# An attention kernel's item loads, with each row of 6144 or 4672 bytes cut into two rows of 3072 or 2368

## The chip, the core and the metric

The program runs on one core of one Trainium2 chip. A core has a matrix engine (PE, with its weight loads shown apart as PEld), a vector engine (DVE), a scalar engine (ACT), a general engine (POOL) and a sequencer that mostly issues transfers (SP). Sixteen DMA engines carry all transfers between the device memory and the on-chip buffers. The metric is the device time of one execution in microseconds (us), taken as the median of the runs.

## The reference

Two blocks follow each other. The first is a linear attention with a decaying state, over 4 batches, 8 heads, 768 tokens and 48 values per head:

```
for t in range(S):
    kt, vt, rt = k[:, :, t], v[:, :, t], r[:, :, t]
    cur = einsum('bhd,bhe->bhde', u * kt, vt)
    y[:, :, t] = einsum('bhd,bhde->bhe', rt, state + cur)
    state = w * state + einsum('bhd,bhe->bhde', kt, vt)
```

The second takes y as x (4 x 768 tokens of 384 values), chooses one of 8 experts for each token by a gate (a token may keep the expert of the token before it), and returns p[e] * (relu(x @ w1[e]) @ w2[e]), where w1 is 384 x 1024 and w2 is 1024 x 384. All is float32.

## The kernel before

The attention takes 16 items, one for each batch and pair of heads (4 x 4). The two heads of an item lie on partitions 0 to 47 and 64 to 111. An item's 768 tokens are six chunks of 128. What an item needs from device memory comes in three loads, which `load(n)` issues on SP's queue:

- `rk`: r and k with the head's values on the partitions and the tokens along them, 128 partitions x 2 x 768 values;
- `kv`: k and v with the tokens on the partitions, 128 partitions x 576 values each and 16 values of padding;
- `vT`: v in a third layout, 128 x 768 values.

Four buffers hold rk and vT, five hold kv. `load(n + 3)` is written ahead of the work of item n, so three items are loaded or under way while one is computed. The loads of items 0, 1 and 2 stand at the very start, those of item 3 follow once the loop begins. Item 0's rk comes in two loads of half the chunks each (L202), every other rk in one (L199); kv is L203, vT is L204. Eight completion counters are used in turn for SP's loads, so an issue also waits until the load eight places before it has landed.

The order of the work on each engine is written by hand in `run`. The steps of an item n, with the lines by which the profile names them:

- POOL, in `scale(n)`: `ke` (L217, k of kv times a table of decays), `rw` (L234, r of rk times decays) and `pd` (L221, r times k), each in two halves. For items 0 to 2 the order is pd, ke and DVE makes rw; from item 3 it is ke, rw, pd. `scale(n + 1)` is issued during item n.
- DVE: `kw` (L241, k of rk times inverse decays), the multiplication of a score by a mask into `am` (L290), the scan over chunk states `S` (L259), the product with vT in `own` (L273), and for the first items two steps L157 and L158 that prepare the inverse decays.
- PE: `added` (L253, ke against v into the bank `mp`), `inside` (L297, am against v), `before` (L310, rw against S), `scores` (L288, rw against kw), `own` (L269, pd summed), `turn` (L323, transposes of the finished item).
- ACT copies results out of the banks (L314, L325) and stores four batches of x to device memory (L328).

After the last load SP fetches the first expert's weights (L1024, L1026). Then ten blocks of tokens run through the experts; PE is busy almost without a break there. Their loads (1536 KB each, rows of 12288 bytes) and the gathers and scatters of tokens on POOL do not touch the tensors of the change.

Of the kernel before, what the change touches and what calls it, by code (L numbers as in the profile page):

```python
# [50 lines left out]
C2 = NCH // 2  # L51
AHEAD = 4
VB = NCH * 2 * DH


def spread(ap, axis, n):
# [5 lines left out]
class Attention:  # L62
# [13 lines left out]
    def __init__(self, tc, st, rk_d, kv_d, vT_d, x_d, w_t, wp_d, kept, ident, lt, mp):  # L76
        self.tc, self.nc = tc, tc.nc
        nc = tc.nc
        self.rk_d, self.kv_d, self.vT_d, self.x_d = rk_d, kv_d, vT_d, x_d
        self.w_t, self.kept, self.ident, self.lt = w_t, kept, ident, lt  # L80

        self.late = st.enter_context(tc.tile_pool(name="late", bufs=1))
        self.wp = self.late.tile([P, H, 32], F32, name="wp")
        self.sel = self.late.tile([P, 2 * (E + 1)], F32, name="sel")
        self.inner = ExitStack()

        def pool(name, bufs, **kw):
            return self.inner.enter_context(tc.tile_pool(name=name, bufs=bufs, **kw))

        once = pool("once", 1)  # L90
        self.two = pool("two", 2)
        self.three = pool("three", 3)
        ps = pool("ps", 1, space=PSUM)

        self.pairs = [ps.tile([P, 2, 512], F32, name=f"pair{i}") for i in range(2)]
        self.py = pool("py", 1, space=PSUM)

        self.T = mp[:, 2 * P + 2:2 * P + 2 + (NCH - 1) * DH].rearrange("p (e c) -> p e c", c=NCH - 1)

        self.inv = pool("pinv", 1, space=PSUM).tile([P, HP, P], F32, name="inv")  # L100


        n = B * HP - 1
        self.rks, self.vTs = [None] * AHEAD, [None] * AHEAD
        for i in range(1, AHEAD + 1):
            self.rks[(n + i) % AHEAD] = once.tile([P, 2, NCH, P], F32, name=f"rk{i}")
        for i in range(1, AHEAD + 1):
            self.vTs[(n + i) % AHEAD] = once.tile([P, 2, C2, P], F32, name=f"vT{i}")
        self.kvs = [once.tile([P, 2 * VB + DP - DH], F32, name=f"kv{i}") for i in range(AHEAD + 1)]
        self.items = [dict() for _ in range(B * HP)]  # L110
        self.xTs, self.xs, self.lTs = {}, {}, {}
        for i in range(AHEAD - 1):
            self.load(i)
        nc.sync.dma_start(out=self.wp, in_=wp_d)


        self.step = once.tile([P, HP, DH, NCH - 1], F32, name="step")
        nc.vector.memset(self.step, 0.0)


        self.tab = tab = once.tile([P, HP, 2, P + 1], F32, name="tab")
        nc.vector.memset(tab[:, 0, :, 0:1], 1.0)
        nc.gpsimd.memset(tab[:, 1:, :, 0:1], 1.0)
        w = once.tile([P, HP, 2], F32, name="w")
        nc.vector.tensor_scalar(w[:, :, 0], w_t[:, :, 0], W_LO, W_HI, Alu.max, Alu.min)
        nc.vector.reciprocal(w[:, :, 1], w[:, :, 0])
        nc.vector.tensor_copy(tab[:, 0, :, 1], w[:, 0])
        nc.gpsimd.tensor_copy(tab[:, 1:, :, 1], w[:, 1:])
        n = 2
        while n <= P:  # L130
            m = min(n - 1, P + 1 - n)
            for engine, t in ((nc.vector, tab[:, :1]), (nc.gpsimd, tab[:, 1:])):
                engine.tensor_mul(t[..., n:n + m], t[..., 1:1 + m], t[..., n - 1:n].to_broadcast([P, t.shape[1], 2, m]))
            n += m

        self.first, self.newton = mp[:, :P + 1], mp[:, P + 1:2 * P + 1]
        nc.scalar.copy(self.first, tab[:, 0, 0])
        self.reciprocals(0)

        self.end = once.tile([P, HP, P + DP], F32, name="end")  # L140
        self.endT = once.tile([P, 2, HP, 2 * DH], F32, name="endT")
        self.align(26)
        self.warm(8)
        self.ends(slice(0, 1))
        self.turn_ends(slice(0, 1))
        self.warm(5)
# [47 lines left out]
    def load(self, n):  # L194
        nc = self.nc
        b, hp = divmod(n, HP)
        rk, vT, kv = self.rks[n % AHEAD], self.vTs[n % AHEAD], self.kvs[n % (AHEAD + 1)]
        if n:
            nc.sync.dma_start(out=rk.rearrange("p a c t -> p (a c t)"), in_=self.rk_d[b, hp])  # L199
        else:  # L200
            for z in (slice(0, C2), slice(C2, NCH)):
                nc.sync.dma_start(out=rk[:, :, z], in_=self.rk_d[b, hp].rearrange("p (a c t) -> p a c t", a=2, c=NCH)[:, :, z])  # L202
        nc.sync.dma_start(out=kv, in_=self.kv_d[b, hp])  # L203
        nc.sync.dma_start(out=vT.rearrange("p a c t -> p (a c t)"), in_=self.vT_d[b, hp])  # L204
        self.items[n].update(b=b, hp=hp, rT=rk[:, 0], kT=rk[:, 1], vT=vT,
                             k=kv[:, :VB].rearrange("p (c x) -> p c x", c=NCH), v=kv[:, VB:])

    def scale(self, n):

# [267 lines left out]
def general_attention(tc, rk_d, kv_d, wu, wg_d, x_d, ident, lt):  # L477

    nc = tc.nc
    with tc.tile_pool(name="g1", bufs=1) as g1, tc.tile_pool(name="g2", bufs=2) as g2, \  # L480
# [9 lines left out]
        with tc.For_i(0, HP, 1) as hp:  # L490
            wu_t = g1.tile([P, 2], F32, name="g_wu")
            nc.sync.dma_start(out=wu_t, in_=wu[bass.ds(hp, 1)].rearrange("o p x -> (o p) x"))
            with tc.For_i(0, B, 1) as b:
                def of(ap):
                    return ap[bass.ds(b, 1), bass.ds(hp, 1)].rearrange("o q p x -> (o q p) x")

                r_t = g1.tile([P, S], F32, name="g_r")
                k_t = g1.tile([P, S], F32, name="g_k")
                v_t = g1.tile([P, NCH, 2, DH], F32, name="g_v")
                nc.sync.dma_start(out=r_t, in_=of(rk_d)[:, :S])  # L500
                nc.sync.dma_start(out=k_t, in_=of(rk_d)[:, S:])
                nc.sync.dma_start(out=v_t.rearrange("p c i e -> p (c i e)"),
                                  in_=of(kv_d)[:, 2 * NCH * DH:4 * NCH * DH])
                yp = gy.tile([P, 2, 512], F32, name="g_y")
                for e in range(DH):
                    vp = gps.tile([P, 2, 512], F32, name="g_vp")
                    for c in range(NCH):
                        for i in range(2):
                            nc.tensor.matmul(
                                vp[i * DP:(i + 1) * DP, c // 3, (c % 3) * P:(c % 3 + 1) * P],  # L510
                                lhsT=v_t[:, c, i, e:e + 1].to_broadcast([P, DP]),
                                rhs=turned if c % 2 else ident,
                                start=True, stop=True)
                    kv = g2.tile([P, S], F32, name="g_kv")
                    nc.vector.tensor_mul(kv.rearrange("p (g t) -> p g t", g=2),
                                         k_t.rearrange("p (g t) -> p g t", g=2), vp[:, :, :3 * P])
                    sv = g2.tile([P, S + 1], F32, name="g_sv")
                    nc.vector.memset(sv[:, 0:1], 0.0)
                    nc.vector.tensor_tensor_scan(sv[:, 1:], wu_t[:, 0:1].to_broadcast([P, S]), kv, 0.0,
                                                 Alu.mult, Alu.add)  # L520
                    z = g2.tile([P, S], F32, name="g_z")
                    nc.vector.scalar_tensor_tensor(z, kv, wu_t[:, 1:2], sv[:, :S], Alu.mult, Alu.add)
                    nc.vector.tensor_mul(z, z, r_t)
                    for c in range(NCH):
                        o = (c % 3) * 2 * DH + 2 * e
                        nc.tensor.matmul(yp[:, c // 3, o:o + 2], lhsT=z[:, c * P:(c + 1) * P], rhs=ones,
                                         start=True, stop=True)
                y = g1.tile([P, 2, 3, 2, DH], F32, name="g_ys")
                for g in range(2):
                    for i in range(2):  # L530
                        nc.vector.tensor_copy(
                            y[:, g, :, i, :],
                            yp[:, g, :6 * DH].rearrange("p (c e i) -> p c e i", c=3, i=2)[:, :, :, i])
                nc.sync.dma_start(
                    out=x_d.rearrange("(b c p) (h j) -> b h p c j", b=B, p=P, h=HP)
                    [bass.ds(b, 1), bass.ds(hp, 1)].rearrange("o q p c j -> (o q p) c j"),
                    in_=y.rearrange("p g c i e -> p (g c) (i e)"))
# [1113 lines left out]
def _rows(a, np):  # L1651

    x = np.pad(a.transpose(0, 1, 3, 2), ((0, 0), (0, 0), (0, DP - DH), (0, 0)))
    return x.reshape(B, HP, P, S)
# [50 lines left out]
```

## Time and profile before

| | |
|---|---|
| three runs | 387.10, 389.02, 388.28 us; median 388.28 |
| profiled execution | 388.15 us, of which the span from first to last instruction is 386.4 |
| busy, share of the span | PE 371.5 us (96%), PEld 328.5 (85%), DVE 247.1 (64%), POOL 151.1 (39%), ACT 107.6 (28%) |
| mean granted clock of PE | 0.997 |
| moved in all | 74.97 MB, 17477 packets, 194 GB/s over the span |
| SP's queue (q1) | 10048 packets, 56.89 MB |
| item loads | 16 kv of 584 KB, 16 vT of 384 KB, 15 rk of 768 KB and 2 of 384 KB |

The attention lasts from the start to about 117 us, the experts from there to the end. In the profile a line such as `POOL ke L217 <- DMA kv<-in_kv_dram` names an engine, the tile it writes and its line, and after the arrow what ended the engine's idle time before it. Lists of waits give the total in us, how many times, and the longest. A timeline line gives the start in us, how long the group lasted, the engine, the line, the operation and its tiles, and in brackets the idle time before it. The DMA share is the packets' time over the time of 16 engines, so it may read a little over 1 where packets overlap.

### The profile page before, as it was taken

The page shows a single profiled execution, that of the slowest core. Times are in us where ns is not written, and L with a number is a line of the kernel's source. Part 1 is how long each engine was busy: PE and PEld are TensorE (multiplying, and loading weights), DVE is VectorE, ACT ScalarE, POOL GpSimd, SP SyncE. Part 2 cuts the span into 40 slices and gives each one's busy share as a digit, 9 for nine tenths or more (in the row PEclk, how much of TensorE's full clock was granted, in tenths as well). Part 3 has the DMA queues.
Part 4 walks back from the last instruction along what each step waited for, and adds up shares of the span by engine and source line. Part 5 has one row for each costly group of instructions (what it writes and reads, how often), then busy time and mean ns, then how long its engine had stood idle before and what let it go on. Part 6 is the DMA issues. An engine that isn't in the chain of part 4 may idle for free. (4 is left out here: it accounts for less than half of the span.)

```text
span 386.4 us, 9723 instructions
## 1 busy us (share of the span) xinstructions
PE 371.5 (96%) x3858; PEld 328.5 (85%) x3858; DVE 247.1 (64%) x718; ACT 107.6 (28%) x293; POOL 151.1 (39%) x212
## 2 busy tenths in 40 slices
PE   7999999799999999999999999999999999999992
PEld 6776877677777999998999999999999999999971
DVE  7887576588954564587657757758757758556400
ACT  4132232222213111322323233234224234222220
POOL 8769998696322022611333222312403213012022
PEclk9999999999999999999999999999999999999998
DMA  7999998979213982740552145245156146064011
GB/s 257 414 409 410 409 405 274 355 256 394 99 32 101 378 338 64 249 185 23 184 179 108 42 170 213 66 171 204 56 185 224 38 165 227 21 199 181 2 37 37
DMA packets 17477, 74.97 MB, mean 194 GB/s; under 512 B 2729, under 2 KB 6586, under 8 KB 14864
## 3 DMA queue, kind: packets, MB, share of 16 engines
q1 hardware_dynamic: 10048, 56.89, 39.1%
q0 software_dynamic: 3424, 9.52, 7.4%
q10 hardware_dynamic: 3952, 7.87, 5.6%
q8 instruction: 32, 0.52, 0.6%
q14 instruction: 21, 0.17, 0.1%
HBM read 64.83 MB, written 9.51 MB: 192 GB/s over the span
## 5 line engine op out<-in xcount | busy, mean ns | idle before, releaser
L1263 POOL DMA_INDIRECT out_dram<-yo,sid x27 | 26.6, 986 | 102.3 <-ACT yo L1258 78.8
L1114 PE MATMUL h<-exT,w1t 128*128 128x168 f32 (+4 forms) x240 | 54.9, 327 | 0.0
L1118 DVE TENSOR_TENSOR hT<-h,hs 128x168 f32<-128x168 f32 (+3 forms) x60 | 21.1, 351 | 46.5 <-PE h L1114 30.4
L1037 POOL DMA_INDIRECT xg<-x_d,gid x29 | 31.1, 1073 | 38.2 <-DVE sm L872 17.4
L1114 PEld LDWEIGHTS h<-exT,w1t 128*128 128x128 f32 x240 | 41.7, 190 | 0.3 <-issue 0.3
L290 DVE TENSOR_TENSOR am<-pair,kept 128x768 f32<-128x768 f32 x32 | 30.1, 952 | 16.8 <-PE pair L288 16.4
L1064 PE MATMUL h<-exT,w1t 128*128 128x192 f32 (+1 forms) x192 | 38.2, 337 | 0.0
L1183 PE MATMUL y<-factors,sums 128*128 128x192 f32 x168 | 36.8, 326 | 0.0
L1114 PE MATMUL h<-xs,ws 128*128 128x168 f32 (+4 forms) x144 | 35.2, 326 | 0.0
L1064 PEld LDWEIGHTS h<-exT,w1t 128*128 128x128 f32 x192 | 32.3, 190 | 1.4 <-issue 0.2
L221 POOL TENSOR_TENSOR pd<-rk 128x384 f32<-128x384 f32 x32 | 31.9, 1017 | 3.0 <-DMA rk<-in_rk_dram 2.2
L297 PE MATMUL y<-am,kv 128*64 128x128 f32 x384 | 28.9, 278 | 3.4 <-issue 2.2
L1114 PEld LDWEIGHTS h<-xs,ws 128*128 128x128 f32 x144 | 25.5, 190 | 4.3 <-ACT hs L1121 1.2
L1183 PEld LDWEIGHTS y<-factors,sums 128*128 128x128 f32 x168 | 28.9, 190 | 0.0
L297 PEld LDWEIGHTS y<-am,kv 128*64 128x64 f32 x384 | 24.8, 136 | 4.7 <-issue 2.4
L234 POOL TENSOR_TENSOR rw<-rk,tab 128x384 f32<-128x384 f32 x26 | 23.6, 931 | 7.3 <-PE y L310 7.3
L217 POOL TENSOR_TENSOR ke<-kv,endT 128x288 f32<-128x288 f32 x32 | 24.9, 799 | 3.9 <-DMA kv<-in_kv_dram 3.0
L314 ACT COPY xT<-y 128x768 f32<-128x768 f32 (+1 forms) x16 | 12.5, 779 | 42.3 <-PE y L310 42.3
L288 PE MATMUL pair<-rw,kw 48*64 48x128 f32 (+1 forms) x768 | 22.4, 249 | 1.3 <-ACT end L168 0.6
L1183 PE MATMUL y<-w2t,hT 128*128 128x192 f32 x96 | 23.0, 328 | 0.0
L1051 DVE COPY exT<-tp 128x384 f32<-128x384 f32 (+6 forms) x29 | 14.0, 489 | 12.8 <-PE tp L1050 12.6
L288 PEld LDWEIGHTS pair<-rw,kw 48*64 48x64 f32 x768 | 19.4, 133 | 2.7 <-issue 0.9
(279 smaller groups left out, 733.0 us busy)
## 6 DMA issues: line engine op xcount, KB each, us to landing
w1t<-in_w_dram SPq DMA_DIRECT2D x9, 1536.0 KB, 6.7
w2t<-in_w_dram SPq DMA_DIRECT2D x9, 1536.0 KB, 7.3
rk<-in_rk_dram SPq DMA_DIRECT2D x15, 768.0 KB, 9.4
kv<-in_kv_dram SPq DMA_DIRECT2D x16, 584.0 KB, 9.1
vT<-in_vT_dram SPq DMA_DIRECT2D x16, 384.0 KB, 7.4
x_d<-x ACTq DMA_DIRECT2D x4, 1152.0 KB, 10.7
w1t<-in_w_dram ACTq DMA_DIRECT2D x1, 1536.0 KB, 10.2
w2t<-in_w_dram ACTq DMA_DIRECT2D x1, 1536.0 KB, 13.5
```

The lines of the kernel that those rows point to most:

```text
L217: nc.gpsimd.tensor_mul(t["ke"][:, p::2], t["k"][:, p::2], spread(self.endT[:, p, hp], 1, C2))
L221: nc.gpsimd.tensor_mul(t["pd"][:, z], t["rT"][:, z], t["kT"][:, z])
L234: engine.tensor_mul(t["rw"][:, z], t["rT"][:, z], spread(pw, 1, z.stop - z.start))
L288: nc.tensor.matmul(sc[f * DP:(f + 1) * DP, h, i, x:], lhsT=t["kw"][q, c, o * DP:(o + 1) * DP], rhs=t["rw"][q, c, x:], start=True, stop=True)
L290: return lambda: nc.vector.tensor_mul(t["am"][:, g], sc, spread(self.kept[:, g:g + 3], 1, 2))
L297: nc.tensor.matmul(t["y"][p * DP:(p + 1) * DP, h, c2 * P:(c2 + 1) * P], lhsT=t["v"][:, (2 * c + h) * DH:(2 * c + h) * DH + DP], rhs=t["am" ...
L1037: self.nc.gpsimd.indirect_dma_start(out=xg[:n], out_offset=None, in_=self.x_d[:rows], in_offset=bass.IndirectOffsetOnAxis(ap=u["gid"][:n, ...
L1064: nc.tensor.matmul(h[:, :n], lhsT=u["w1"][:, m, kk, :], rhs=u["xT"][:, kk, :], start=(kk == 0), stop=(kk == DK - 1))
L1114: nc.tensor.matmul(out, lhsT=a, rhs=b, start=start and k == 0, stop=stop and k == len(terms) - 1, skip_group_check=True)
L1118: nc.vector.tensor_tensor(out, a, b, op=Alu.add)
L1183: return lambda: nc.tensor.matmul(bank[:, x * half:(x + 1) * half], lhsT=a, rhs=b, start=(j == 0 and x == 0), stop=(j == FK // 2 - 1), ski ...
L1263: self.nc.gpsimd.indirect_dma_start(out=out.rearrange("n (h d) -> (n h) d", h=2) if half else out, out_offset=bass.IndirectOffsetOnAxis(ap ...
```

## The change

In device memory r and k (and k and v of the token-wise tensor) no longer stand side by side in a partition's row; each is a plane of its own, of 128 rows. A load still fills the same partition row on the chip, from two places. An rk row of 6144 bytes becomes two of 3072, and a kv row of 4672 becomes two of 2368: the padding of 16 values now follows k as well as v, so a kv tile is 64 bytes wider on each partition. The number of loads, their order, their waits, and every compute instruction stay as they are. Item 0's rk was and is read in rows of 1536 bytes, four to a partition. vT is not changed. The slow path `general_attention`, which this input does not enter, reads the planes too.

```diff
+VW = VB + DP - DH
...
-        self.kvs = [once.tile([P, 2 * VB + DP - DH], F32, name=f"kv{i}") for i in range(AHEAD + 1)]
+        self.kvs = [once.tile([P, 2, VW], F32, name=f"kv{i}") for i in range(AHEAD + 1)]
...
         if n:
-            nc.sync.dma_start(out=rk.rearrange("p a c t -> p (a c t)"), in_=self.rk_d[b, hp])
+            nc.sync.dma_start(out=rk.rearrange("p a c t -> p a (c t)"), in_=self.rk_d[b, hp].rearrange("a p x -> p a x"))
         else:
             for z in (slice(0, C2), slice(C2, NCH)):
-                nc.sync.dma_start(out=rk[:, :, z], in_=self.rk_d[b, hp].rearrange("p (a c t) -> p a c t", a=2, c=NCH)[:, :, z])
-        nc.sync.dma_start(out=kv, in_=self.kv_d[b, hp])
+                nc.sync.dma_start(out=rk[:, :, z], in_=self.rk_d[b, hp].rearrange("a p (c t) -> p a c t", c=NCH)[:, :, z])
+        nc.sync.dma_start(out=kv, in_=self.kv_d[b, hp].rearrange("a p x -> p a x"))
         nc.sync.dma_start(out=vT.rearrange("p a c t -> p (a c t)"), in_=self.vT_d[b, hp])
         self.items[n].update(b=b, hp=hp, rT=rk[:, 0], kT=rk[:, 1], vT=vT,
-                             k=kv[:, :VB].rearrange("p (c x) -> p c x", c=NCH), v=kv[:, VB:])
+                             k=kv[:, 0, :VB].rearrange("p (c x) -> p c x", c=NCH), v=kv[:, 1])
...
-        "rk": _np.concatenate([_rows(i["r"], _np), _rows(i["k"], _np)], 3),
-        "kv": _np.pad(_np.concatenate([_tokens(i["k"], _np), _tokens(i["v"], _np)], 3),
-                      ((0, 0), (0, 0), (0, 0), (0, DP - DH))),
+        "rk": _np.stack([_rows(i["r"], _np), _rows(i["k"], _np)], 2),
+        "kv": _np.pad(_np.stack([_tokens(i["k"], _np), _tokens(i["v"], _np)], 2), ((0, 0),) * 4 + ((0, DP - DH),)),
```

More of the change, by code (lines that the diff above doesn't have):

```diff
@@ L493, in general_attention, with of @@
             with tc.For_i(0, B, 1) as b:
-                def of(ap):
-                    return ap[bass.ds(b, 1), bass.ds(hp, 1)].rearrange("o q p x -> (o q p) x")
+                def of(ap, a):
+                    return ap[bass.ds(b, 1), bass.ds(hp, 1)].rearrange("o q a p x -> a (o q p) x")[a]
                 r_t = g1.tile([P, S], F32, name="g_r")
@@ L499, in general_attention @@
                 v_t = g1.tile([P, NCH, 2, DH], F32, name="g_v")
-                nc.sync.dma_start(out=r_t, in_=of(rk_d)[:, :S])
-                nc.sync.dma_start(out=k_t, in_=of(rk_d)[:, S:])
+                nc.sync.dma_start(out=r_t, in_=of(rk_d, 0))
+                nc.sync.dma_start(out=k_t, in_=of(rk_d, 1))
                 nc.sync.dma_start(out=v_t.rearrange("p c i e -> p (c i e)"),
-                                  in_=of(kv_d)[:, 2 * NCH * DH:4 * NCH * DH])
+                                  in_=of(kv_d, 1)[:, :VB])
                 yp = gy.tile([P, 2, 512], F32, name="g_y")
```

## The prediction

> **What bounds the kernel now.** I read the page first, for where the transfers are dense:
>
> ```profile
> DMA  7999998979213982740552145245156146064011
> GB/s 257 414 409 410 409 405 274 355 256 394 99 32 101 378 338 64 249 185 23 184 179 108 42 170 213 66 171 204 56 185 224 38 165 227 21 199 181 2 37 37
> ```
>
> A slice is 9.66 us. From the second to the sixth the DMA engines are full, at 405 to 414 GB/s: the item loads. So the loads are the scarce thing in the first 58 us, and the question is whether anyone waits for them. The chain of work that ended last is no help: it holds one scatter. So next the waits, POOL's and DVE's between 3 and 35 us:
>
> ```profile
> POOL ke L217 <- DMA kv<-in_kv_dram: 3.0, 1, 3.0
> POOL pd L221 <- DMA rk<-in_rk_dram: 2.2, 2, 1.2
> DVE am L290 <- PE pair L288: 2.3, 3, 1.8
> DVE y L273 <- PE y L269: 1.5, 3, 0.6
> DVE mp L157 <- PE mp L253: 0.6, 1, 0.6
> ```
>
> POOL alone waits for loads, three times, 5.2 us in all: for rk of items 1 and 2 (at 11.49 and 15.95 us) and for kv of item 3 (at 22.41). Over the whole span the list of waits has no other computing engine behind an item load. DVE waits for PE only. Whether POOL's wait matters is read from the timeline around the latest of them:
>
> ```profile
> 22.41 1.56 POOL L217 TENSOR_TENSOR ke<-kv,endT 128x288 f32<-128x288 f32 x2 [3.00 <-DMA kv<-in_kv_dram]
> 23.93 1.69 POOL L234 TENSOR_TENSOR rw<-rk,tab 128x384 f32<-128x384 f32 x2
> 25.57 1.97 POOL L221 TENSOR_TENSOR pd<-rk 128x384 f32<-128x384 f32 x2
> 27.50 1.57 POOL L217 TENSOR_TENSOR ke<-kv,endT 128x288 f32<-128x288 f32 x2
> ...
> 24.12 0.64 DVE L259 TENSOR_TENSOR_SCAN S<-step,mp 128x240 f32<-128x240 f32 x1
> 24.83 0.56 PEld L253 LDWEIGHTS mp<-kv,ke 128*48 128x48 f32 x20 [0.60 <-POOL rw L234]
> 26.22 0.95 DVE L241 TENSOR_TENSOR kw<-rk,inv 128x768 f32<-128x768 f32 x1
> 27.32 1.23 PEld L288 LDWEIGHTS pair<-rw,kw 48*64 48x64 f32 x47
> 28.65 0.24 PEld L269 LDWEIGHTS y<-pd,w_t 48*64 48x64 f32 x8
> ```
>
> ke of item 3 ends at 23.97, and its reader, `added` on PE (L253), starts at 24.83. The view names POOL's rw as releaser, but `added` does not read rw. It overwrites the bank `mp` that DVE's scan S of item 2 reads until 24.76: that is the releaser. So ke(3) has 24.76 - 23.97 = 0.79 us to spare. rw(3) ends at 25.62 and is read at 27.32, after kw (1.6 us to spare); pd(3) ends at 27.54 and is read at 28.65 (1.1); ke(4) ends at 29.07, `added(4)` starts at 30.21 (1.1). In this stage DVE and PE set the pace by each other, and POOL, though fed late, is in time.
>
> **The change part by part.** Every instruction of the computing engines stays in place, with its waits. What changes is 31 loads (15 rk, 16 kv): on each of 16 engines 8 partition rows, each now two packets.
>
> The price of a packet comes from the packet records of SP's queue (medians): 12288 bytes 460 ns, 6144 bytes 234, 4672 bytes 180, 3072 bytes 121, 1536 bytes 65. These lie on a line: 8 ns and 0.0368 ns a byte. The 3072 is vT's own packet, on the same queue, in the same microseconds, and so the nearest row that there can be. So an rk row goes from 234 to 2 x 121 = 242 ns (+8). A kv row goes from 180 to 2 x (8 + 0.0368 x 2368) = 2 x 95 = 190 (+10, of which 2 are the 64 bytes of padding). An item takes 8 x (234 + 180 + 121) = 4.28 us of each engine before, and 8 x (242 + 190 + 121) = 4.42 after: 3.4% more.
>
> Ahead of the moment that decides, the landing of kv(3), stand the changed loads kv(0), rk(1), kv(1), rk(2), kv(2), rk(3), kv(3) in one queue that is full all the time: 8 x (4 x 10 + 3 x 8) = 512 ns. kv(3) was issued at 11.44 and took 10.8 us:
>
> ```profile
> kv<-in_kv_dram SPq DMA_DIRECT2D x1, 584.0 KB, 10.8
> ```
>
> It lands at 22.24, and would at 22.75. ke(3) then ends at 24.48, still 0.28 before 24.76. POOL's following steps move by 0.51 and keep 0.6 to 1.1 us. On the path: nothing. If this cover were gone, PE would move by what is over.
>
> Bounds of the price. Below: in windows of 10 us between 10 and 50 the DMA share reads 1.02 to 1.03, so packet times overlap by 2 to 3%; with some 28 packets per engine in 5 us that is 3 to 5 ns each, and the added packet may cost 3 ns instead of 8. Still fewer is excluded, since the bytes do not fall. Above: the dearest small packets in the trace are item 0's first 1536-byte ones, with a mean of 111 ns against 65 between 2.5 and 3.0 us, 46 more. At 54 ns each the 56 packets ahead (7 loads x 8 rows) cost 3.0 us, 2.2 beyond the cover. I take 8, since vT's packets are the same size at the same time, and keep 3 and 54 for the range: 0 to +2.2 us.
>
> The Trainium skill (DMA: Bandwidth & Descriptors, section "Why small descriptors are slow (HBM only)") gives a packet a fixed overhead of about 3 cycles on the engines' inner bus beside one cycle per 32 bytes, and counts it a loss at 256 bytes. By that, as an estimate, 6144 bytes in two packets are 198 cycles for 195, or 1.5%, where the rows above give 3.4%; kv(3) would land about 0.25 us later and the end would not move either.
>
> The other items. kv(4) lands at 26.60 for a ke that starts at 27.50, kv(5) at 30.81 for 33.25, kv(6) at 35.19 for 38.61, kv(7) at 39.39 for 44.22, and from there about 5 us are left each time. The added 0.14 us per item is small beside that, and POOL moves too. An item takes about 6 us (`before` starts at 46.62, 52.56, 58.75), its loads 4.4 us of each DMA engine and a quarter of a store of x at 1152 KB, at most 0.8: the loads cannot become the bound there. vT(0) lands at 9.52 for a step at 10.23, moves by 0.08. kv(0) lands at 8.59 for ke(0) at 8.70, whose reader starts at 10.88, 0.6 us after ke's end.
>
> SP. An issue of a 256-packet load may be longer: the two of item 0's rk took 1.32 us together, against a median of 0.33 for others, so up to 0.34 more. Behind it on SP stand only loads. kv(3) was issued when rk(1) landed, eight places before, and then lay 10.8 us in the queue, so 0.34 is lost in the backlog. The first weights, last in SP's line, land at 94.0 and 98.7, and PE first reads them at 119.4.
>
> The sum: 388.15 (386.4 of span and 1.75 around it) + 0. That execution is 0.13 under the median of the three. With that, and 0.1 for kv(0), which falls in the first microseconds where packets are dear, I say 388.4.
>
> **The rivals.** *Slower: the two planes cost rate, not packets.* A row now comes from two places, 384 KiB apart for rk, and every engine alternates between them. No load in the trace reads like that, so nothing excludes it. The item 0 loads, also in pieces, ran at 304 to 351 GB/s between 3 and 8 us (windows), against 410 later, though that is also the start of all traffic. From 2.0 us, where traffic starts, to 22.24 the queue runs 20.2 us. The cover of 0.79 is used up at a loss of 3.9%, where the sum above already has 2.5. Each further per cent costs 0.2 us, and over 1.94 us (0.5% of the time, about what a measurement of this kernel can tell from no change) needs 13.5%. At the first microseconds' 330 for 410 GB/s, 20% less, kv(3) is 5 us late and the end about 4.3: 392.5.
>
> The Trainium skill (same page, section "Latency and other measured facts") has rates that fall by 3% at a row pitch of 512 KiB and to half at 4 MiB. No run here shows that, and the pitch here is between two planes and not between partitions; 3% taken on top would make about +0.3 us.
>
> *Faster: smaller packets let loads land sooner.* Were every one of POOL's waits for loads gone, 5.2 us of idle POOL time would go, and behind it stands only one wait, DVE's 0.6 us before L157 at 11.81 (it waits for `added(0)`, that for ke(0), that for kv(0)). So -0.6 at most: 387.7, no difference to a measurement. More would have to come from where the loads aren't.
>
> *It does nothing:* the packets could be joined again. The planes are not adjacent in memory, so a row cannot be one packet; if it were, the time would be 388.2.
>
> **How the numbers follow.** No difference (the sum, with the packet price anywhere from 3 ns to about 45): 0.62, with its own range 387.2 to 389.9, from the spread of three runs (387.10 to 389.02) and the shift. The planes or the packets cost more than that: 0.28, at 390.3 to 392.6. Faster by over 0.5%: 0.10, for what the trace cannot show, since no wait there supports it. The range for 8 in 10 is 387.0 to 392.0: half of the slower case lies inside.
>
> **What would show it.** Right: in the changed profile, rk and kv packets of 3072 and 2368 bytes at 121 and 95 ns, 31 x 128 = 3968 more packets in SP's queue (14016 for 10048); POOL's wait before ke(3) about 3.0 + 0.2 us (it starts waiting later by 0.3); L217 of item 3 at 22.9 and L253 still at 24.8; the DMA line unchanged in slices 2 to 6 or fuller after them. Wrong: L253 of item 3 later than 25.1 with POOL's ke as the last releaser; GB/s under 380 in those slices; a DMA wait of PE or DVE in the list; or a step of the experts that lasts longer.

## The result, and the profile after

Ten runs each: 391.70 us median after (388.69 to 393.09) against 387.49 before (386.12 to 389.02). The ratio is 1.0099, with a 95% interval of 1.0073 to 1.0124: 1% slower. The profiled execution took 391.67 us, of which 389.9 are span. (The runs of before were three when the prediction was made, with a median of 388.28.) In each round of experiments before ran again on the same chip, with a median of 386.84 to 387.18; every ratio below is to that before, with its 95% interval, and one run over 1.5% above its kernel's fastest (394.7 us) is left out of its ratio.

The page's lines for transfers over 40 slices, and its line for SP's queue (packets, MB, share of 16 engines), after:

```profile
DMA  8999998899501984651534145155146145054011
GB/s 280 399 400 397 314 368 286 300 332 383 200 13 43 356 347 146 226 197 32 173 114 171 51 168 203 53 185 207 54 171 235 38 164 214 32 189 187 2 36 36
```

```profile
q1 hardware_dynamic: 14016, 57.02, 40.0%
```

The packets are as forecast: 14016 on SP's queue, and in the packet records 122 ns for 3072 bytes and 95 for 2368. In slices 2 to 4 the queue is full as before and moves some 3% less. So the change did what it says. In slices 5 and 6 it moves 314 and 368 GB/s, under the 380 that the prediction named as a sign of being wrong; the experiments show that this goes with a late start and not with the packets. Now three of the waits of POOL and DVE between 3 and 35 us:

```profile
POOL ke L218 <- DMA kv<-in_kv_dram: 1.7, 1, 1.7
POOL tab L129 <- DVE w L127: 2.2, 1, 2.2
DVE w L126 <- DMA w_t<-in_wu_dram: 2.8, 1, 2.8
```

POOL waits less for loads than before, not more. (DVE has one wait of 0.3 us behind an item load.) New at the top is a wait that has nothing to do with the items: DVE waits for `w_t`, the decay rates, a load of 4 KB that ACT issues at the start. Every table that scales r and k is computed from it. Its reader on DVE's timeline, before and then after:

```profile
2.79 0.17 DVE L125 TENSOR_SCALAR w<-w_t 128x4 f32<-128x4 f32 x1 [0.83 <-DMA w_t<-in_wu_dram]
```

```profile
4.80 0.17 DVE L126 TENSOR_SCALAR w<-w_t 128x4 f32<-128x4 f32 x1 [2.84 <-DMA w_t<-in_wu_dram]
```

and the load in the list of DMA issues (the last number is us from issue to landing), before and then after:

```profile
w_t<-in_wu_dram ACTq DMA_DIRECT2D x1, 4.0 KB, 1.9
```

```profile
w_t<-in_wu_dram ACTq DMA_DIRECT2D x1, 4.0 KB, 4.0
```

The load lands 2.1 us later, and the first step starts 2.0 us later. Why can be read from the first issues of the two queues, before and then after:

```profile
0.82 1.32 SPq L202 DMA_DIRECT2D rk<-in_rk_dram  x2
0.82 0.43 ACTq L1581 DMA_DIRECT2D w_t<-in_wu_dram  x1
```

```profile
0.82 0.96 SPq L203 DMA_DIRECT2D rk<-in_rk_dram  x2
0.82 0.49 ACTq L1582 DMA_DIRECT2D w_t<-in_wu_dram  x1
```

Both queues start at 0.82 us. (The lines of SP give both rk loads together, with the gap between them.) Before, the first of item 0's two rk loads takes 0.67 us to issue and w_t's 0.43, and w_t is first: its 512 packets of 8 bytes run from 1.89 to 2.42 us, those of rk from 2.35. After, rk's issues are shorter, 0.45 and 0.46, ACT's takes 0.49, and rk is first: its packets run from 1.91, those of w_t from 2.90 to 4.18, in between rk's of 1536 bytes, which take 65 ns each (median). The Trainium skill (DMA: Bandwidth & Descriptors, section "Queues, rings and completion order") says that a DMA engine takes turns between the queues at packets. The trace agrees that they mix: from 2.90 to 4.18 us, 272 packets of rk start among the 512 of w_t. Why w_t's first packet comes 0.99 us after rk's first, turns alone do not say.

The wait does not end at 2 us. The matmuls of item 0, from 7 to 14 us, before and after:

```profile
L288 PE MATMUL pair<-rw,kw 48*64 48x128 f32 x48 | 1.7, 277 | 0.6 <-ACT end L168 0.6
L269 PE MATMUL y<-pd,w_t 48*64 48x384 f32 x8 | 0.8, 482 | 0.0
```

```profile
L289 PE MATMUL pair<-rw,kw 48*64 48x128 f32 x48 | 2.8, 422 | 0.0
L270 PE MATMUL y<-pd,w_t 48*64 48x384 f32 x8 | 1.5, 844 | 0.0
L175 PE MATMUL pair<-ident,end 128*128 128x128 f32 x4 | 1.4, 448 | 1.4 <-ACT end L168 1.4
```

The same matmuls take 1.5 to 1.75 times as long after, until about 14 us, and the last line shows PE idle for 1.4 us before L175, PE's first step that needs w. The views print a granted clock of 1.00 for these windows in both, but that is no reading: the trace's record of the clock has its first entry, full speed, at 4.92 us in before and at 14.32 in after, and the views count the time ahead of it as full. The scan S of item 0, before and then after:

```profile
12.36 0.64 DVE L259 TENSOR_TENSOR_SCAN S<-step,mp 128x240 f32<-128x240 f32 x1
```

```profile
16.54 0.64 DVE L260 TENSOR_TENSOR_SCAN S<-step,mp 128x240 f32<-128x240 f32 x1
```

Of these 4.18 us, 2.0 are w_t; the other 2.2 go with the slow matrix engine, as an experiment below shows. Then the distance stays, from item to item: 4.18 through item 4, 4.26 at 5 and 6, 5.27 from 7 to 10, 3.62 at 11 and 3.51 at the last.

### The profile page after: what moved, and what is told of

It reads as the page before. It is cut to its first block, busy times and chain, and to the rows that moved or that the text cites. A ratio compares the mean times of both kernels' runs of the same rounds, so it can differ in the third digit from the quotient of the medians.

```text
span 389.9 us, 9723 instructions
## 1 busy us (share of the span) xinstructions
PE 374.9 (96%) x3858; PEld 331.2 (85%) x3858; DVE 246.9 (63%) x718; ACT 107.6 (28%) x293; POOL 151.7 (39%) x212
## 3 DMA queue, kind: packets, MB, share of 16 engines
q1 hardware_dynamic: 14016, 57.02, 40.0%
## 5 line engine op out<-in xcount | busy, mean ns | idle before, releaser
L289 PE MATMUL pair<-rw,kw 48*64 48x128 f32 (+1 forms) x768 | 23.6, 258 | 0.9 <-issue 0.6
L289 PEld LDWEIGHTS pair<-rw,kw 48*64 48x64 f32 x768 | 20.6, 139 | 2.2 <-issue 1.0
```

Of the source, the lines that this page charges most:

```text
L289: nc.tensor.matmul(sc[f * DP:(f + 1) * DP, h, i, x:], lhsT=t["kw"][q, c, o * DP:(o + 1) * DP], rhs=t["rw"][q, c, x:], start=True, stop=True)
```

## The experiments

**Theory A**: the loss comes from when w_t lands, and that from item 0's rk being read from planes; PE at a lower pace adds to it. **Theory B**: the 31 loads with more packets cost load rate, and the loss is theirs.

### The change by parts

Four kernels, each with a part of the change. The diffs show the loads that differ from before (in the fourth from after); the lines that lay out inputs and tiles to match are left out.

*Only kv in planes* (rk as before):

```diff
-        nc.sync.dma_start(out=kv, in_=self.kv_d[b, hp])
+        nc.sync.dma_start(out=kv, in_=self.kv_d[b, hp].rearrange("a p x -> p a x"))
```

> Only kv in planes (4096 packets of 2368 bytes), rk in rows as before. Theory A (item 0's rk, read from planes, gets ahead of the small load of w_t, so the first step that needs w, DVE L125, starts at 4.8 us in place of 2.8, and the matrix engine then stays at the lower clock): nothing of this is here, w_t lands as before, DVE L125 at 2.8, time within 0.8 us of before. Theory B (the added packets cost load rate and the attention gets its loads late): kv carries 16 x 8 x 10 of the 2350 ns of added packet time on each engine, over half, so about +2 us.

Measured: ratio 1.0016 (0.9991 to 1.0040), no change. DVE's first step on w at 3.31 us in its profile, S of item 0 at 12.88: a little over what A expected (w_t's last packet started at 2.86). By the prediction's prices the added packet time is 16 x 80 + 15 x 64 = 2240 ns, not 2350; kv's share is over half either way.

*Only rk in planes*, item 0's among them:

```diff
-            nc.sync.dma_start(out=rk.rearrange("p a c t -> p (a c t)"), in_=self.rk_d[b, hp])
+            nc.sync.dma_start(out=rk.rearrange("p a c t -> p a (c t)"), in_=self.rk_d[b, hp].rearrange("a p x -> p a x"))
...
-                nc.sync.dma_start(out=rk[:, :, z], in_=self.rk_d[b, hp].rearrange("p (a c t) -> p a c t", a=2, c=NCH)[:, :, z])
+                nc.sync.dma_start(out=rk[:, :, z], in_=self.rk_d[b, hp].rearrange("a p (c t) -> p a c t", c=NCH)[:, :, z])
```

> Only rk in planes, item 0 among them; kv in rows as before. Theory A: the whole loss, +3.5 to +4.2 us, with DVE's first step on w at about 4.8 us. Theory B: the smaller half, about +1.7 us, with that step at 2.8.

Measured: 1.0142 (1.0119 to 1.0165), the whole loss and a little more; first step on w at 4.85. Here the record of the clock begins early enough to show the matrix engine. Its transposes were quick (272 ns) from 5.75 us, it then idled 1.79 us, and from 9.11 to 15.94 us the granted clock was a half and the matmuls of item 0's scores took 420 ns. The page's line has it in the second slice:

```profile
PEclk9699999999999999999999999999999999999997
```

*Before, with item 0's rk alone in planes*, from an input of its own:

```diff
-                nc.sync.dma_start(out=rk[:, :, z], in_=self.rk_d[b, hp].rearrange("p (a c t) -> p a c t", a=2, c=NCH)[:, :, z])
+                nc.sync.dma_start(out=rk[:, :, z], in_=self.rk0_d.rearrange("a p (c t) -> p a c t", c=NCH)[:, :, z])
```

> Before, with nothing but item 0's rk read from planes, from an input tensor of its own; its packets are 1536 bytes as they were, and no packet is added anywhere. Theory A: the whole loss, +3.5 to +4.2 us, w's first step at about 4.8. Theory B: no packet more, so 0 (within 0.8 us).

Measured: 1.0086 (1.0053 to 1.0119). No packet was added, none changed its size, and the loss is there, with the late first step on w:

```profile
4.68 0.17 DVE L126 TENSOR_SCALAR w<-w_t 128x4 f32<-128x4 f32 x1 [2.72 <-DMA w_t<-in_wu_dram]
```

Three of its eight runs lie at 388.4 to 388.9, four at 391.2 to 393.1 and one at 394.7.

*After, with item 0's rk alone in rows*, all 31 other loads in planes:

```diff
-                nc.sync.dma_start(out=rk[:, :, z], in_=self.rk_d[b, hp].rearrange("a p (c t) -> p a c t", c=NCH)[:, :, z])
+                nc.sync.dma_start(out=rk[:, :, z], in_=self.rk0_d.rearrange("p (a c t) -> p a c t", a=2, c=NCH)[:, :, z])
```

> After, with item 0's rk read from rows as before, from an input tensor of its own; all 31 other loads in planes. Theory A: as before, within 0.8 us, with w's first step at 2.8. Theory B: the whole loss, +3.5 to +4.2 us.

Measured: 1.0003 (0.9983 to 1.0024), with every added packet in place. Its first step on w, and its rates over the slices:

```profile
2.79 0.17 DVE L127 TENSOR_SCALAR w<-w_t 128x4 f32<-128x4 f32 x1 [0.83 <-DMA w_t<-in_wu_dram]
```

```profile
GB/s 253 403 400 399 402 405 335 357 283 350 120 32 116 364 355 49 254 182 23 185 206 82 42 178 219 54 171 205 69 172 225 37 166 234 15 204 176 2 37 37
```

Slices 2 to 6 run at 399 to 405 GB/s here, with all the added packets; the third kernel, with none, has 313 and 354 in slices 5 and 6. The third and fourth kernel settle it: the loss goes with item 0's two loads and not with the 31.

### The order of the two first loads

w_t issued on SP ahead of item 0's rk, so that one queue orders them, in after and in before:

```diff
-    nc.scalar.dma_start(out=w_t, in_=wu.rearrange("h p x -> p h x"))
+    nc.sync.dma_start(out=w_t, in_=wu.rearrange("h p x -> p h x"))
```

> After, but the load of w_t is issued on SP's queue ahead of item 0's rk and not on ACT's queue beside it, so that nothing decides between the two but the order on one queue. Theory A: w's first step on DVE back at about 2.8 us, the time within 0.8 us of before. Rival B (the planes of the 31 loads cost something that shows only with item 0's rk in planes too): still +2 us or more over before, with that step at 2.8.

> Before, with w_t's load first on SP's queue in the same way. Theory A: w_t already came first, so no change, within 0.8 us; together with the after kernel of the same edit it gives the price of the planes alone, forecast 0 to 0.3 us. If the edit itself is worth something, this kernel is faster than before by it.

Measured against the same before: 0.9988 (0.9966 to 1.0010) for after, 0.9987 (0.9965 to 1.0008) for before. With the order held, planes or rows make no difference. These two also show the price of the packets alone. The load of kv of item 3 in the lists of DMA issues, in the kernel in rows and then in the one in planes, both with w_t first:

```profile
kv<-in_kv_dram SPq DMA_DIRECT2D x1, 584.0 KB, 10.6
```

```profile
kv<-in_kv_dram SPq DMA_DIRECT2D x1, 592.0 KB, 11.8
```

and its two readers in their timelines, in the same order:

```profile
22.61 1.54 POOL L217 TENSOR_TENSOR ke<-kv,endT 128x288 f32<-128x288 f32 x2 [2.72 <-DMA kv<-in_kv_dram]
24.88 0.56 PEld L253 LDWEIGHTS mp<-kv,ke 128*48 128x48 f32 x20 [0.59 <-issue]
```

```profile
23.24 1.56 POOL L218 TENSOR_TENSOR ke<-kv,endT 128x288 f32<-128x288 f32 x2 [3.21 <-DMA kv<-in_kv_dram]
24.94 0.56 PEld L254 LDWEIGHTS mp<-kv,ke 128*48 128x48 f32 x20 [0.59 <-POOL ke L218]
```

Issued at 11.86 and 11.31, it lands at 22.46 and 23.11: 0.65 us later. ke follows, 0.63 later, and ends at 24.80. `added` starts 0.06 later, as much as the scan S of item 2 ahead of it, which now ends at 24.87. (The last line names ke as the releaser; the scan ended later.) So the cover held, and 0.07 us of it is left.

*Before, with w_t behind item 0's rk* on SP, all rows as they were:

```diff
-    nc.scalar.dma_start(out=w_t, in_=wu.rearrange("h p x -> p h x"))
...
+        if n == 0:
+            nc.sync.dma_start(out=self.w_t, in_=self.wu.rearrange("h p x -> p h x"))
         nc.sync.dma_start(out=kv, in_=self.kv_d[b, hp])
```

> Before, all rows as they were, but w_t's load issued on SP's queue behind the two loads of item 0's rk. Theory A: w_t lands after them at about 5 us, w's first step on DVE moves from 2.8 to about 5.2, and the loss is at least as large as the one of after: +3.5 to +5.5 us, with not one packet changed. Theory B: 0, since the loads' packets are those of before.

Measured: 1.0146 (1.0108 to 1.0184), 6.2 us between the medians and more than expected. The first step on w is at 5.84 us, PE then idles 2.79 us before its L175 and runs slowly after:

```profile
9.22 0.69 PE L175 MATMUL pair<-ident,end 128*128 128x128 f32 x2 [2.79 <-ACT end L168]
10.90 2.84 PE L291 MATMUL pair<-rw,kw 48*64 48x128 f32 x48
```

S of item 0 comes 6.44 us later than before: 3.05 for w, 3.4 for PE. The loss can be made with no change of layout at all.

### The matrix engine's part

After, with PE kept busy in the gap:

```diff
-        self.warm(8)
+        self.warm(15)
```

> After, with 15 in place of 8 idle transposes while the matrix engine waits for the tables of w (warm), which fill its 1.45 us of idle time before L175. If the loss is 2.0 us of waiting for w_t and some 2 us of a matrix engine left at the lower clock by that gap, the second part shrinks: matmuls of item 0's scores at 270 ns and not 417, the time 1.5 to 2.3 us under after, some 2 us over before. If the lower clock has another cause than the gap, the time stays that of after.

Measured: 1.0028 (1.0005 to 1.0051). w still comes late (first step at 4.94), but the matmuls are quick again:

```profile
L289 PE MATMUL pair<-rw,kw 48*64 48x128 f32 x48 | 1.7, 277 | 0.6 <-ACT end L169 0.6
L270 PE MATMUL y<-pd,w_t 48*64 48x384 f32 x8 | 0.8, 482 | 0.0
```

S of item 0 is 2.15 us late in place of 4.18. So about half of the early loss was the wait, and the other half a matrix engine at a lower pace after its work had stopped: in after's profile it had not come up to speed before that, in that of *only rk in planes* it had, and lost it again. The end came out better than expected: 1.35 us over before, where some 2 were forecast.

### What orders the two loads

w_t laid out as 32 bytes to a partition, so that its load is 128 packets and not 512 of 8 bytes; still on ACT's queue in the first two, first on SP's in the third:

```diff
-    nc.scalar.dma_start(out=w_t, in_=wu.rearrange("h p x -> p h x"))
+    nc.scalar.dma_start(out=w_t, in_=wu)
...
-        "wu": _np.stack([w, u.reshape(HP, P)], 2),
+        "wu": _np.stack([w, u.reshape(HP, P)], 2).transpose(1, 0, 2),
```

> After, with w_t laid out so that its load, still on ACT's queue, is 128 packets of 32 bytes and not 512 of 8. Theory A says what costs is when w_t lands. If the load whose issue is done first is served first, a shorter issue on ACT (under the 0.48 us of item 0's rk from planes) puts w_t first: DVE's first step on w at 2.7 us or before, time within 0.8 us of before. If item 0's rk from planes is served first whatever w_t's length, w_t's packets start at 2.9 us as in after but are a quarter as many: that step at 3.3 to 3.7, time 0.5 to 1.5 us over before.

Measured for after with that: 1.0018 (0.9994 to 1.0041), the loss gone within what the runs can tell. Its issue lines:

```profile
0.81 0.97 SPq L203 DMA_DIRECT2D rk<-in_rk_dram  x2
0.82 0.42 ACTq L1582 DMA_DIRECT2D w_t<-in_wu_dram  x1
```

ACT's issue is 0.42 us and so under the 0.45 of SP's first, and w_t's packets run from 1.85 us, rk's from 1.98. The first step on w is at 2.87, not under 2.7. That agrees with "the issue that is done first is served first", as do all the profiles with both loads on two queues: 0.38 to 0.43 against 0.67 (w_t first, four times), 0.49 against 0.45 (rk first, four times). It is not shown that the issue's length is the cause; another property of the plane form could shorten both. Nor does a load's own form alone set the length: kv of item 0, issued next, takes 0.59 us behind rows and 0.46 behind planes, whichever form it has itself.

> Before, with w_t's load in the same 128 packets of 32 bytes on ACT's queue. w_t lands first in any case; with 8 packets an engine in place of 32 at 9 ns each, 0.2 to 0.4 us earlier, so DVE's first step on w at 2.4 to 2.6 us and the time 0 to 0.4 us under before, which the rounds can hardly tell.

> Before, with w_t in 128 packets and its load first on SP's queue: the shortest and the first. DVE's first step on w at 2.4 to 2.6 us, item 0's rk later by the 0.33 to 0.45 us of that issue, time 0 to 0.6 us under before. If the matrix engine's lower clock at the start, and not w, then sets the pace, no gain.

Measured: 0.9990 (0.9970 to 1.0009) and 0.9994 (0.9973 to 1.0016). In both the first step on w comes at 2.44 us, 0.35 earlier, and S of item 0 0.2 earlier. No version beats before by more than the runs can tell.

## Why the prediction was right or wrong

The likeliest case of the prediction, no difference at 388.4, did not come; 391.7 lies in the range and in the time that the slower rival gave, but not for its reason: that the range holds it is luck. Three of its signs of being wrong came: a DMA wait of DVE, slices under 380 GB/s, and `added` of item 3 later than 25.1 us, at 29.01, with ke named as releaser. With w_t first and all loads in planes they do not come (`added` at 24.94, slices at 399 to 406), but for DVE's wait for w_t, which before has too.

- **Packet prices: right.** 121 and 95 ns forecast, 122 and 95 measured.
- **The landing of kv(3): right, a little small.** 0.51 us forecast, 0.65 with the order of the first loads held; POOL's wait before ke was forecast at 3.2 us and is 3.21 there. In after itself POOL is later when it begins to wait, and waits 1.74, so only the pair with w_t first shows this.
- **The cover of 0.79 us: right.** No time was lost at the deciding `added`, nor later; the 31 loads in planes cost 1.0003 (0.9983 to 1.0024).
- **The rival of slower planes: wrong.** Its rate loss of over 13% did not come: with all 31 loads in planes and item 0's rk in rows, slices 2 to 6 move 399 to 405 GB/s for 405 to 414. What it took for a sign, item 0's loads at 304 to 351 GB/s, says nothing for it: in after, with planes, the same microseconds have 322 to 411.
- **The step that failed** is "Every instruction of the computing engines stays in place, with its waits. What changes is 31 loads". The two loads of item 0 change too: packets as before, but from addresses with which the first issue takes 0.45 us for 0.67. The sum had no term for them, nor for w_t, which shares the DMA engines and whose landing starts the chain of tables. The SP paragraph looked only for a longer issue and for what stands behind it on SP, and not for what stands beside it on ACT's queue. And the list of waits was read from 3 us on, and over the whole span for item loads only, which left out the one DMA wait that sat on the path, DVE's 0.83 us before 2.79. So "POOL alone waits for loads" and "DVE waits for PE only" do not hold for the start. In their place the runs showed w_t landing 2.1 us later and the slow matrix engine behind it, 4.18 us at the first scan.
- **The second missing term** is the matrix engine's pace. The prediction took matmuls at their durations. The Trainium skill (TensorE: Matmul & The Clock Gate, Part 1) has the array at half clock until it was busy for a window of about 3.4 us that runs freely against the program. The trace agrees in kind: transposes of 272 ns in before from about 4.9 us, 421 in after until 14. In the profiles with w_t early PE was quick by about 7 us, and also with 15 transposes in the gap; four profiles have an entry of half clock before the program's end, of 3.41 or 6.83 us. By that page, as an estimate, one window more at half clock costs up to 1.7 us. The traces have a loss of 2.0 to 3.4 us, and the first entry of full speed comes 9.4 us later in after than in before, more than one window.
- **From 4.18 us at item 0 to 3.5 at the end**: PE waits 0.9 us at 52 us in after for no releaser that the profile shows, and a like wait of 2.16 us before L297 at 74 in before is 0.51 in after. From item 9 to item 11 the profiles of the experiments move by -2.8 to +1.7 us against before's. In all thirteen profiles every wait of PE of over 0.5 us after 25 us ends 1.2 to 1.6 us after a 16 KB transfer on the queue that the page calls instruction (before: transfer done at 72.69, PE on at 74.03; after: 50.72 and 52.23). So PE may have waited for its own program; no run tests it. In three profiles the granted clock falls to a half around such a wait, in the last experiment's from 74.13 to 77.55 us, where 1.7 us are lost. What share of the change from 4.18 to 3.5 these make stays open.

That some runs of item 0's rk alone come out near 388.5 would follow if PE kept its speed across the gap in those; no profile fell on one, so it is only argued. To have come up to speed before the gap is not enough, as the profile of *only rk in planes* shows, at 391.5 us.

## What to carry to other kernels

Before a load's layout is changed, list all loads in flight with it on every queue, the few-byte ones first, and ask who starts a chain on them: two queues that issue at the same moment have an order, and here it turned where the issues differed by a few hundredths of a microsecond. Where one load starts everything, issue it first on the same queue, or make it few packets; either edit made this kernel indifferent to the layout, within what the runs can tell. Read the list of waits from zero, and where the matrix engine idles early, look at the mean of its matmuls, since a granted clock of 1.00 can stand for a time that the clock's record does not cover.

## What the runs showed of the hardware that was not expected

- The first load of 2 x 384 values to a partition took 0.66 to 0.67 us to issue on SP when its source pieces lay in one row and 0.45 to 0.50 when they lay in two planes, with the same number and size of packets, in every profile.
- 4 KB in 512 packets of 8 bytes landed 1.9 us after issue when served first and 4.0 when behind the start of a 384 KB load; in 128 packets of 32 bytes, and first, DVE used it 0.35 us sooner.
- An idle gap of 1.4 us at 6.4 us, before the matrix engine had come up to speed, was followed by matmuls of 422 ns for 277 until 14 us. In another profile the engine was at speed from 5.70 us, and a gap of 1.8 us was followed by half the granted clock from 9.11 to 15.94.
